# Conversion guards of attention-time weights moved to GpSimd in two steps, with shifts and joinings behind a unit's first maximum

## The chip, the cores and the metric

The kernel runs on one core of one Trainium2 chip. A time is device microseconds (us) of that core for one execution of the whole program. The number that is compared is the median over several executions: 718.2 us for the kernel before, from three runs (719.97, 717.71 and 718.2). The profile is of another execution of the same program, whose own time was 719.17 us.

## The reference

Three operators stand one behind the other.

```python
# 1. attention over 2 batches x 8 heads, 768 tokens, head size 64
q_bucket, k_bucket = sum over 6 bits of ((q @ proj > 0) * 2**bit), the same for k
mask = q_bucket[:, :, :, None] == k_bucket[:, :, None, :]
scores = np.where(mask, scale * q @ k.T, -1e9)
scores = scores - np.max(scores, axis=-1, keepdims=True)
attn = np.exp(scores); attn = attn / (attn.sum(-1) + 1e-9)
x = attn @ v                          # to 1536 tokens x 512
# 2. gated product, d_ff = 1536
x = (x @ w_a) * (x @ w_b) @ w_out
# 3. router and 8 experts, one expert for each token, d_ff = 1024
logits = normalised(x) @ normalised(expert_emb).T / tau
out[t] = gate[t] * relu(x[t] @ w1[e]) @ w2[e]      # e = argmax of the logits of token t
```

The weights reach the chip as 64-bit floats, in pairs of 32-bit words, and are made into two 32-bit parts (a high one and a small low one) on the chip. The products of stage 2 with the activations' high and low parts use them.

## The kernel before

**Stages.** Attention fills about the first 224 us of the span, the gated product runs from there to about 518 us, and the router and the experts fill the rest. The order of the instructions on each engine is written out by hand: Python code issues the work in program order, and each engine runs its own instructions in that order. The Tile layer adds the semaphore waits between engines.

**Attention.** The work is cut into 48 units (`units`): 8 pairs of heads, two heads in a pair, three groups of 256 queries in a head. The loop `for u in range(NU + 2)` issues, for unit u, in this order: the first row maximum on VectorE (`rowmax(u, 0)`, L278), its exponential on ScalarE (`expo`, L284), the reciprocal of the sums of the unit before (`recip(u - 1)`, L288, VectorE), the second maximum (`rowmax(u, 1)`), the normalising of the unit before (`normal(u - 1)`: a small `s` on VectorE in L294, a small `mc` and two 128x768 products `e` on GpSimd in L293 and L296), the first scores of the next unit on TensorE, the second exponential, the preparation of later heads, the transposing of unit u - 2 on VectorE (`turn`, L303), the second scores of the next unit, and a third of a head's product with the values (`pv`, L315). The scores live in a PSUM pool of two buffers, so the scores of a half wait for the exponential of the half two back.

**Hooks.** At fixed places of a unit the loop calls `hook(u, at)`: `at` 3 stands ahead of `turn`, 2 behind it, 0 behind the value products, 1 behind the loading of values, and 4 at the unit's end. A dictionary `plan` says what is issued there.

**Weights converted during attention.** The first two slices of `w_a`, `w_b` and `w_out` are converted while attention runs. `load_first` calls `split64`, which gives a `fetch` (a DMA on SyncE, L487) and seven steps: `rest` (a shift on VectorE, L492), `top` (a joining on VectorE, L495), `low` (ScalarE, L501), `add` (GpSimd, L506), `size` (ScalarE, L511), `guard` (VectorE, L517: the value is kept where its low word is large enough, else zero) and `parts` (a cast on ScalarE in L522, a subtraction on GpSimd in L523). `jobs[0..3]` are `w_a` and `w_b` of slice 0 and of slice 1, `outs[0..1]` are `w_out`. The table `places` names the unit of each of the seven steps of each job; `low` has m = 2, `guard` m = 5. The steps with m of 3, 4 and 6 stand at hook 3, the others at hook 4. The four jobs share the two buffers of `spare`, so that job 2 takes job 0's buffer and job 3 takes job 1's; the outs share the one buffer `late`.

**Fill-in products.** `fill` puts the first products of stage 2 into units 40, 43, 46, 47, 48, 51 and 52. Two halves of a product add up in one PSUM bank. Those of units 51 and 52 are read from their banks by ScalarE or VectorE (L601, L605) ahead of the first output product `yp` (L624), which takes the next bank in turn.

**Router.** For each token tile, `transpose_in` (T) turns the tile, and its eight logits come from a chain of products `lgp` (`route_logits`, R, L713) or, for three tiles at once, from one product `lgt` (`group_logits`, GL, L725) and three transposes `lgu` (`group_turn`, GT, L735). Tiles 9 to 11, the last ones, have T and R in a hand-written chain.

Of the kernel before, what the change touches and what calls it, by code (L numbers as in the profile page):

```python
# [25 lines left out]
class Kernel:  # L26
# [37 lines left out]
    def attention(self, xh, xl, pools, hook):  # L64
        nc = self.nc
# [306 lines left out]
        for u in range(NU + 2):  # L372
# [10 lines left out]
            if 0 <= u - 1 < NU:  # L383
                recip(u - 1)
            if act:
                rowmax(u, 1)
# [21 lines left out]
            if new < len(pairs):  # L408
                preps, held, held_kind = [kind(new, x) for x in (1, 0)], new, kind
# [46 lines left out]
class Experts:  # L456
# [16 lines left out]
    def split64(self, src, shape, dest, scratch=None):  # L473
# [40 lines left out]

        def guard():
            v = f32(T["v"])
            nc.vector.scalar_tensor_tensor(v, f32(T["lo"]), 2.0 ** -15, v, ALU.is_ge, ALU.mult)  # L517
# [7 lines left out]
        return fetch, [rest, top, low, add, size, guard, parts]  # L525
# [30 lines left out]
    def load_first(self, which, f, scratch):  # L556
# [15 lines left out]
        return self.split64(src, shape, dest, scratch)  # L572
# [145 lines left out]
    def group_logits(self, t):  # L718

        nc = self.nc  # L720
        yt = self.yT[t]
        q = self.rt.tile([128, 512], F32, tag="rt", name="lgt")
        for k in range(self.KD):
            rows = slice(32 * k, 32 * k + 32)
            nc.tensor.matmul(q[rows, :384], self.enT[:, k], yt[:, k], start=True, stop=True)  # L725
        ls = self.LS = self.sb.tile([128, self.DM], F32, tag="sq", name="lgs", bufs=1)
        nc.scalar.copy(ls[:, :384], q[:, :384])

    def group_turn(self, t):
# [4 lines left out]
        for m in range(3):  # L734
            nc.tensor.transpose(q[:, m * 128:(m + 1) * 128], self.LS[:, m * 128:(m + 1) * 128], self.K.ident)  # L735
        parts = q[:, :384].rearrange("p (m k e) -> p m e k", k=self.KD, e=32)
        nc.vector.tensor_reduce(self.lg[b][:, c:c + 3], parts[:, :, :self.E], axis=AX.X, op=ALU.add)
# [349 lines left out]
def tile_kernel(ctx, tc, q, k, v, proj, w_a, w_b, w_out, emb, tau, w1, w2, out, dbg=None):  # L1087
# [5 lines left out]
    with tc.manual_schedule():  # L1093
# [15 lines left out]
        with tc.tile_pool(name="conv", bufs=1, side="left") as X.conv, \  # L1109
# [7 lines left out]
            def late():  # L1117
                return sb.tile([128, 2 * S], F32, tag="raw", name="late", bufs=1)

            jobs = [X.load_first(w, f, spare) for f in range(2) for w in range(2)]  # L1120
            outs = [X.load_first(2, f, late) for f in range(2)]


            plan = {(-1, 0): [jobs[0][0], jobs[1][0]], (35, 1): [outs[0][0]], (45, 1): [outs[1][0]]}
            places = (
                (3, 4, 5, 6, 6, 7, 9), (8, 8, 9, 10, 12, 13, 15), (16, 17, 18, 21, 21, 22, 27), (20, 23, 24, 28, 30, 31, 33),
                (37, 38, 39, 40, 41, 41, 45), (NU, NU + 1, NU + 1, NU + 2, NU + 2, NU + 2, NU + 3),
            )
            for (_, steps), us in zip(jobs + outs, places):
                for m, u in enumerate(us):  # L1130
                    plan.setdefault((u, 3 if m in (3, 4, 6) else 4), []).append(steps[m])
            plan[13, 0], plan[16, 0] = [jobs[2][0]], [jobs[3][0]]
# [7 lines left out]
            def hook(u, at):  # L1140
# [5 lines left out]
                if at == 0:  # L1146
                    for n in range(fill.get(u, 0)):
                        t, f, w, half = first.pop(0)
                        if half == 0:
# [194 lines left out]
```

## Time and profile before

| | us |
|---|---|
| median of three runs | 718.2 |
| the profiled execution | 719.17 |
| its span (first to last instruction) | 717.3 |

| engine | busy us | share of the span | instructions |
|---|---|---|---|
| PE (TensorE) | 695.9 | 97% | 6802 |
| DVE (VectorE) | 463.8 | 65% | 672 |
| POOL (GpSimd) | 415.2 | 58% | 343 |
| ACT (ScalarE) | 354.8 | 49% | 659 |

The shares are means over three stages that differ. The clock granted to TensorE was 0.999 of full speed over the span. In rows of a timeline the first two numbers are the start and the duration in us; a bracket at the end is the idle time ahead of the instruction and what ended it. In rows that group instructions, the numbers behind the bar are the busy time in us, the mean of one in ns, and the idle time ahead with its releasers.

### The profile page before, as it was taken

What the parts mean: (1) busy time and instruction counts of PE and PEld (TensorE: products, weight loads), DVE (VectorE), ACT (ScalarE), POOL (GpSimd) and SP (SyncE); (2) the same over time, 40 slices, a digit from 0 to 9 for tenths busy, and PEclk for the clock granted to TensorE, in tenths of its full rate; (3) what the DMA queues carried; (4) which work ended last, traced back from release to release, by engine and by line L of the source; (5) the groups of instructions that cost most, each with busy time, mean ns of one, the idle gap of its engine ahead of it and who ended that gap; (6) DMA issues with size and microseconds to landing.
All of it is one profiled execution on the core that took longest, in us unless ns stands there. A gap on an engine that the chain in (4) does not pass through costs nothing.

```text
span 717.3 us, 16210 instructions
## 1 busy us (share of the span) xinstructions
PE 695.9 (97%) x6802; PEld 584.6 (82%) x6802; DVE 463.8 (65%) x672; ACT 354.8 (49%) x659; POOL 415.2 (58%) x343
## 2 busy tenths in 40 slices
PE   8799999999999999999999999999999999999996
PEld 5355655666688999999999999998899899989995
DVE  4999999999974726546556556325645766556650
ACT  4778888888663441121212112143546566556560
POOL 0658778887864645645626627454425666657651
PEclk9999999999999999999999999999999999999999
DMA  6947646644241311111302201633432866576510
GB/s 153 206 105 168 160 116 135 156 113 108 47 134 60 120 60 58 59 59 59 97 22 69 109 0 59 225 113 103 163 107 81 278 232 203 205 255 236 201 47 24
DMA packets 68443, 87.99 MB, mean 123 GB/s; under 512 B 28931, under 2 KB 41027, under 8 KB 68368
## 3 DMA queue, kind: packets, MB, share of 16 engines
q1 hardware_dynamic: 63728, 78.41, 37.5%
q0 software_dynamic: 2560, 7.34, 2.7%
q10 hardware_dynamic: 2080, 1.18, 0.6%
q8 instruction: 54, 0.88, 0.5%
q14 instruction: 21, 0.17, 0.1%
HBM read 75.52 MB, written 7.34 MB: 116 GB/s over the span
## 4 chain that ended last, share of the span: by engine, by line
PE 79%; DVE 11%; ACT 4%; issue 3%; DMA 3%; POOL 0%; SPq 0%; POOLq 0%; DVEq 0%
PE ab L592 25%; PE yp L624 14%; PE op L968 11%; PE hp L918 10%; PE pv L315 6%; DVE nm L278 5%; PE st L270 4%; DVE et L303 4%; ACT e L284 2%; PE hr L936 2%; PE part L592 2%; PE st L273 1%; PE xgt L895 1%; PE pv L592 1%; DMA late<-in_moe_w_out_dram 1%
## 5 line engine op out<-in xcount | busy, mean ns | idle before, releaser
L592 PE MATMUL ab<-xh,w 128*128 128x384 f32 x704 | 185.7, 338 | 0.0
L592 PEld LDWEIGHTS ab<-xh,w 128*128 128x128 f32 x704 | 127.7, 188 | 2.0 <-issue 1.2
L296 POOL TENSOR_SCALAR e<-e,s,mc 128x768 f32<-128x768 f32 x96 | 93.5, 984 | 43.0 <-ACT e L284 33.0
L592 PE MATMUL ab<-xl,w 128*128 128x384 f32 x352 | 118.3, 336 | 0.0
L607 POOL TENSOR_TENSOR g<-a,g 128x384 fp32r<-128x384 f32 x48 | 53.5, 1115 | 102.4 <-ACT g L606 102.4
L874 POOL TENSOR_TENSOR w<-raw,w 128x1024 fp32r<-128x1024 f32 x36 | 88.2, 2454 | 37.2 <-ACT w L873 35.7
L624 PE MATMUL yp<-w,g 128*128 128x512 f32 x432 | 103.0, 391 | 0.7 <-DVE a L605 0.7
L284 ACT ACTIVATE e<-st,nm 128x768 f32<-128x768 f32 x96 | 85.8, 899 | 32.4 <-DVE r L288 22.2
L278 DVE TENSOR_REDUCE nm<-st 128x1 f32<-128x768 f32 x96 | 89.6, 938 | 8.9 <-PE st L273 8.4
L624 PEld LDWEIGHTS yp<-w,g 128*128 128x128 f32 x432 | 80.3, 188 | 15.9 <-DVE a L605 1.0
L270 PE MATMUL st<-ks,qs 64*128 64x384 f32 x192 | 83.2, 513 | 5.4 <-ACT e L284 5.4
L270 PE MATMUL st<-k,q 64*128 64x384 f32 x192 | 83.8, 517 | 3.6 <-ACT e L284 3.3
L303 DVE STREAM_TRANSPOSE et<-e 128x1536 f32<-128x1536 f32 x48 | 84.9, 1769 | 0.0
L968 PE MATMUL op<-w,hth 128*128 128x512 f32 x256 | 80.8, 397 | 0.0
L918 PE MATMUL hp<-xgh,w 128*128 128x256 f32 x448 | 80.7, 281 | 0.0
L606 ACT CAST g<-a 128x384 fp32r<-128x384 f32 x48 | 24.7, 515 | 111.0 <-DVE a L605 111.0
L874 DVE TENSOR_TENSOR w<-raw,w 128x1024 fp32r<-128x1024 f32 x28 | 67.4, 2406 | 13.5 <-ACT w L873 13.5
L315 PEld LDWEIGHTS pv<-et,vr 32*64 32x64 f32 x3072 | 60.2, 130 | 18.2 <-issue 9.4
L315 PE MATMUL pv<-et,vr 32*64 32x192 f32 x3072 | 72.5, 326 | 2.3 <-ACT q L128 1.6
L918 PEld LDWEIGHTS hp<-xgh,w 128*128 128x128 f32 x448 | 69.2, 188 | 0.3
L601 ACT COPY a<-ab 128x384 f32<-128x384 f32 x44 | 21.0, 478 | 95.3 <-PE ab L592 94.1
L629 DVE TENSOR_TENSOR y<-yp,y 128x512 f32<-128x512 f32 x60 | 41.5, 692 | 39.2 <-PE yp L624 39.2
(217 smaller groups left out, 1260.4 us busy)
## 6 DMA issues: line engine op xcount, KB each, us to landing
raw<-in_moe_w_dram SPq DMA_DIRECT2D x32, 1024.0 KB, 5.4
vr<-in_v_dram SPq DMA_DIRECT2D x64, 192.0 KB, 3.8
raw<-in_moe_w_a_dram SPq DMA_DIRECT2D x5, 1024.0 KB, 5.0
raw<-in_moe_w_b_dram SPq DMA_DIRECT2D x5, 1024.0 KB, 5.1
raw<-in_moe_w_out_dram SPq DMA_DIRECT2D x5, 1024.0 KB, 5.0
raw<-in_k_dram SPq DMA_DIRECT2D x16, 192.0 KB, 4.0
qs<-q SPq DMA_DIRECT2D x15, 192.0 KB, 3.8
raw<-in_q_dram SPq DMA_DIRECT2D x14, 192.0 KB, 4.3
```

The lines of the kernel that those rows point to most:

```text
L270: nc.tensor.matmul(st[:, n, :H2], q[d, ql], k[d], start=True, stop=False, tile_position=(64 * n, 0))
L278: nc.vector.tensor_reduce(NM[u][:, t:t + 1], ST[u, t][:, :, :H2], axis=AX.XY, op=ALU.max, negate=True)
L284: nc.scalar.activation(halves(E[u][:, t]), ST.pop((u, t))[:, :, :H2], AF.Exp, bias=NM[u][:, t:t + 1], accum_out=SU[u][:, t:t + 1])
L296: nc.gpsimd.tensor_scalar(E[u][:, t], E[u][:, t], r[:, t:t + 1], c[:, t:t + 1], ALU.mult, ALU.add)
L303: nc.vector.transpose(ET[h][:, :, 2 * g:2 * g + 2].rearrange("p b c s -> p c b s"), E.pop(u).rearrange("p c (b s) -> p c b s", s=32),)
L315: nc.tensor.matmul(pvb[a // 2][m:m + 64, a % 2, :NC * 32], v[d], et[d, n].rearrange("p c s -> p (c s)"), start=(n < 2), stop=(n >= NB32 - ...
L592: nc.tensor.matmul(p[:, :384], w[:, k, fs], x[:, k, cols], start=(k == 0 and n == 0), stop=(k == self.KD - 1 and n == 2),)
L607: nc.gpsimd.tensor_tensor(gl[:, f], a, f32(gh[:, f]), ALU.subtract)
L624: nc.tensor.matmul(p, g[:, f, rows], w[:, f], start=(n == 0), stop=(n == 5))
L874: eng.tensor_tensor(l, raw, f32(h), ALU.subtract)
L918: nc.tensor.matmul(p[:, :256], w[:, k, fs], x[:, k], start=(n == 0), stop=(n == 3 * self.KD - 1))
L968: nc.tensor.matmul(p, h[:, 2 * n + f, rows], w[:, f], start=(n == 0 and f == 0 and m == 0), stop=(n == 3 and f == 1 and m == 2),)
```

## The change

The guard of the weights that are converted during attention gets another form where its engine is GpSimd: `mask` turns the low word into 0 or 1 in place, and `guard` multiplies the value by it. Five of the six guards take this form; that of `outs[1]` stays on VectorE. A new hook 5 stands between the reciprocal and the second maximum, and `rest` and `top` go there. The table `places` has eight columns and other units. The fetch of job 3 goes from hook 0 of unit 16 to hook 0 of unit 21, and that of `outs[1]` from (45, 1) to (46, 1). The two preparations of signs are issued in the other order. One more PSUM bank is taken ahead of the products of unit 51. In the router, tiles 9 and 10 get their logits from one `group_logits` of 256 columns and two transposes in the place of two `route_logits`.

```diff
--- before.py
+++ after.py
@@ -382,6 +382,7 @@
                 expo(u, 0)
             if 0 <= u - 1 < NU:
                 recip(u - 1)
+            hook(u, 5)
             if act:
                 rowmax(u, 1)
             if 0 <= u - 1 < NU:
@@ -406,7 +407,7 @@
             if u + 1 < NU:
                 scores(u + 1, 1)
             if new < len(pairs):
-                preps, held, held_kind = [kind(new, x) for x in (1, 0)], new, kind
+                preps, held, held_kind = [kind(new, x) for x in ((1, 0) if kind is turned else (0, 1))], new, kind
             elif s != 1 and u >= 5:
                 n = (u - 5) % 3
                 pv((u - 5) // 3, range(12 * n, 12 * n + 12))
@@ -470,7 +471,7 @@
         self.yT, self.sel, self.mx, self.rps, self.HS, self.RW = ({} for _ in range(6))
 
 
-    def split64(self, src, shape, dest, scratch=None):
+    def split64(self, src, shape, dest, scratch=None, eng=None):
 
         nc = self.nc
         n = shape[0] * shape[1]
@@ -512,8 +513,15 @@
             else:
                 nc.vector.tensor_scalar(T["lo"], T["hi"], 0x7FFFFFFF, None, ALU.bitwise_and)
 
+        def mask():
+            if eng is nc.gpsimd:
+                eng.tensor_scalar(f32(T["lo"]), f32(T["lo"]), 2.0 ** -15, 1.0, ALU.is_ge, ALU.mult)
+
         def guard():
             v = f32(T["v"])
+            if eng is nc.gpsimd:
+                eng.tensor_tensor(v, v, f32(T["lo"]), ALU.mult)
+                return
             nc.vector.scalar_tensor_tensor(v, f32(T["lo"]), 2.0 ** -15, v, ALU.is_ge, ALU.mult)
 
         def parts():
@@ -522,7 +530,7 @@
             nc.scalar.copy(h, v)
             nc.gpsimd.tensor_tensor(l, v, f32(h), ALU.subtract)
 
-        return fetch, [rest, top, low, add, size, guard, parts]
+        return fetch, [rest, top, low, add, size] + ([mask] if eng else []) + [guard, parts]
 
     def parts(self, shape):
 
@@ -553,7 +561,7 @@
             jobs.append(self.split64(src[:, rows], (n, shape[1]), dest, scratch))
         return jobs
 
-    def load_first(self, which, f, scratch):
+    def load_first(self, which, f, scratch, eng):
 
         K = self.K
         w32 = [w.bitcast(I32) for w in (K.w_a, K.w_b, K.w_out)][which]
@@ -569,7 +577,7 @@
                 self.WG[0, which] = self.parts(whole)
             return [t[:, :, 128 * f:128 * f + 128] if which < 2 else t[:, f:f + 1] for t in self.WG[0, which]]
 
-        return self.split64(src, shape, dest, scratch)
+        return self.split64(src, shape, dest, scratch, eng)
 
 
     def gated_products(self, c, t, f, which, half, psum=None, held=None):
@@ -715,26 +723,27 @@
             )
         nc.vector.tensor_copy(self.lg[b][:, c], q[:, :self.E])
 
-    def group_logits(self, t):
-
-        nc = self.nc
-        yt = self.yT[t]
+    def group_logits(self, t, m=3):
+
+        nc = self.nc
+        n = 128 * m
+        yt = self.yT[t][:, :, :n]
         q = self.rt.tile([128, 512], F32, tag="rt", name="lgt")
         for k in range(self.KD):
             rows = slice(32 * k, 32 * k + 32)
-            nc.tensor.matmul(q[rows, :384], self.enT[:, k], yt[:, k], start=True, stop=True)
+            nc.tensor.matmul(q[rows, :n], self.enT[:, k], yt[:, k], start=True, stop=True)
         ls = self.LS = self.sb.tile([128, self.DM], F32, tag="sq", name="lgs", bufs=1)
-        nc.scalar.copy(ls[:, :384], q[:, :384])
-
-    def group_turn(self, t):
+        nc.scalar.copy(ls[:, :n], q[:, :n])
+
+    def group_turn(self, t, n=3):
 
         nc = self.nc
         b, c = divmod(3 * t, self.TB)
         q = self.rt.tile([128, 512], F32, tag="rt", name="lgu")
-        for m in range(3):
+        for m in range(n):
             nc.tensor.transpose(q[:, m * 128:(m + 1) * 128], self.LS[:, m * 128:(m + 1) * 128], self.K.ident)
-        parts = q[:, :384].rearrange("p (m k e) -> p m e k", k=self.KD, e=32)
-        nc.vector.tensor_reduce(self.lg[b][:, c:c + 3], parts[:, :, :self.E], axis=AX.X, op=ALU.add)
+        parts = q[:, :128 * n].rearrange("p (m k e) -> p m e k", k=self.KD, e=32)
+        nc.vector.tensor_reduce(self.lg[b][:, c:c + n], parts[:, :, :self.E], axis=AX.X, op=ALU.add)
 
     def wide(self, t):
         return t.rearrange("p (t e) -> p t e", e=1).to_broadcast([128, self.TB, self.E])
@@ -1117,19 +1126,20 @@
             def late():
                 return sb.tile([128, 2 * S], F32, tag="raw", name="late", bufs=1)
 
-            jobs = [X.load_first(w, f, spare) for f in range(2) for w in range(2)]
-            outs = [X.load_first(2, f, late) for f in range(2)]
-
-
-            plan = {(-1, 0): [jobs[0][0], jobs[1][0]], (35, 1): [outs[0][0]], (45, 1): [outs[1][0]]}
+            jobs = [X.load_first(w, f, spare, nc.gpsimd) for f in range(2) for w in range(2)]
+            outs = [X.load_first(2, f, late, (nc.gpsimd, nc.vector)[f]) for f in range(2)]
+
+
+            plan = {(-1, 0): [jobs[0][0], jobs[1][0]], (35, 1): [outs[0][0]], (46, 1): [outs[1][0]]}
             places = (
-                (3, 4, 5, 6, 6, 7, 9), (8, 8, 9, 10, 12, 13, 15), (16, 17, 18, 21, 21, 22, 27), (20, 23, 24, 28, 30, 31, 33),
-                (37, 38, 39, 40, 41, 41, 45), (NU, NU + 1, NU + 1, NU + 2, NU + 2, NU + 2, NU + 3),
+                (3, 4, 5, 6, 6, 6, 7, 9), (9, 10, 12, 15, 15, 15, 16, 21),
+                (16, 21, 21, 22, 24, 24, 27, 33), (22, 27, 27, 28, 30, 30, 34, 39),
+                (37, 38, 39, 40, 41, 41, 45, 46), (NU, NU + 1, NU + 1, NU + 2, NU + 2, NU + 2, NU + 2, NU + 3),
             )
             for (_, steps), us in zip(jobs + outs, places):
                 for m, u in enumerate(us):
-                    plan.setdefault((u, 3 if m in (3, 4, 6) else 4), []).append(steps[m])
-            plan[13, 0], plan[16, 0] = [jobs[2][0]], [jobs[3][0]]
+                    plan.setdefault((u, 3 if m in (3, 4, 7) or m == 6 and u < NU else 5 if m < 2 and u < NU else 4), []).append(steps[m])
+            plan[13, 0], plan[21, 0] = [jobs[2][0]], [jobs[3][0]]
             first = [(t, f, w, h) for t in range(2) for f in range(2) for w in range(2) for h in range(2)]
 
 
@@ -1147,6 +1157,8 @@
                     for n in range(fill.get(u, 0)):
                         t, f, w, half = first.pop(0)
                         if half == 0:
+                            if (u, n) == (NU + 3, 0):
+                                K.bank()
                             X.part = K.banks[(2, 0)[n // 2]] if u < NU - 1 else K.bank()
                         X.gated_products(0, t, f, w, half, X.part, held if u < NU + 2 else None)
 
@@ -1287,7 +1299,7 @@
         after(("o", L, 3, 0), X.transpose_in, 0, 0)
         after(("o", L, 3, 0), X.gather, 1, 0)
         chain(("o", L, 3, 1), [
-            (T, 9), [(T, 10), (R, 9)], [(T, 11), (X.route_norm, 1), (R, 10)], [(R, 11), (X.route_choose, 1)],
+            (T, 9), (T, 10), [(T, 11), (GL, 3, 2), (X.route_norm, 1)], [(R, 11), (GT, 3, 2), (X.route_choose, 1)],
         ])
         after(("t", 0, 0, 0), X.route_places, 1)
         chain(("e", 0, 0, 0), [[(X.route_slots, 1), (X.gather, 0, 1)]])
```

**VectorE, units 21 to 23.** Here `spare_1270` (before) and `spare_1640` (after) are job 3's buffer, `spare_1055` and `spare_1054` are job 2's. `nm` is the pair of maxima of a unit, of which each has two rows. Before, from the first maximum of unit 20:

```order
L278 TENSOR_REDUCE nm_1486<-st_1458 128x1 [waits PE_49]
L288 RECIPROCAL r_1491<-su_1446 128x2 [waits Activation_49]
L278 TENSOR_REDUCE nm_1486<-st_1471 128x1 [waits PE_49]
L294 SCALAR_TENSOR_TENSOR s2_1495<-nm_1444,r_1491 128x2 [waits DVE_49]
L303 STREAM_TRANSPOSE et_1512<-e_1364 128x2x24x32 [waits Pool_49]
L492 TENSOR_SCALAR spare_1270<-spare_1270 128x512 [waits DMAHW5_49]
L278 TENSOR_REDUCE nm_1569<-st_1500 128x1 [waits PE_49]
L288 RECIPROCAL r_1574<-su_1488 128x2 [waits Activation_49]
L278 TENSOR_REDUCE nm_1569<-st_1514 128x1 [waits PE_49]
L294 SCALAR_TENSOR_TENSOR s2_1578<-nm_1486,r_1574 128x2 [waits DVE_49]
L303 STREAM_TRANSPOSE et_1512<-e_1447 128x2x24x32 [waits Pool_49]
L278 TENSOR_REDUCE nm_1650<-st_1583 128x1 [waits PE_49]
```

After, from the first maximum of unit 21:

```order
L278 TENSOR_REDUCE nm_1562<-st_1494 128x1 [waits PE_49]
L288 RECIPROCAL r_1567<-su_1482 128x2 [waits Activation_49]
L496 SCALAR_TENSOR_TENSOR spare_1054<-spare_1054 128x512
L278 TENSOR_REDUCE nm_1562<-st_1508 128x1 [waits PE_49]
L294 SCALAR_TENSOR_TENSOR s2_1572<-nm_1480,r_1567 128x2 [waits DVE_49]
L303 STREAM_TRANSPOSE et_1506<-e_1441 128x2x24x32 [waits Pool_49]
L278 TENSOR_REDUCE nm_1649<-st_1577 128x1 [waits PE_49]
L288 RECIPROCAL r_1654<-su_1564 128x2 [waits Activation_49]
L493 TENSOR_SCALAR spare_1640<-spare_1640 128x512 [waits DMAHW3_49,Pool_49]
L278 TENSOR_REDUCE nm_1649<-st_1587 128x1 [waits PE_49]
L294 SCALAR_TENSOR_TENSOR s2_1659<-nm_1562,r_1654 128x2 [waits DVE_49]
L303 STREAM_TRANSPOSE et_1506<-e_1483 128x2x24x32
```

Before, job 3's shift follows the transpose of unit 20 and waits for its load alone. After, job 3's shift stands between the two maxima of unit 22 (`nm_1649`) and waits for its load and for GpSimd; job 2's joining stands in unit 21.

**SyncE, around job 3's load.** `vr` are values, `qg` the query signs, `raw` keys and queries of a later pair. Before:

```order
L94 DMA vr_1219<-in_v_dram 32x4x384 [waits DMAHW4_49]
L487 DMA spare_1270<-in_moe_w_b_dram 128x4x256 [waits DMAHW5_49,DVE_49,Pool_49]
L87 DMA raw_1293<-in_k_dram 128x6x64 [waits DMAHW6_49,PE_49]
L87 DMA raw_1293<-in_q_dram 128x6x64 [waits DMAHW7_49]
L87 DMA raw_1293<-in_k_dram 128x6x64 [waits DMAHW0_49]
L87 DMA raw_1293<-in_q_dram 128x6x64 [waits DMAHW1_49]
```

After:

```order
L240 DMA qg_1471<-qf_1470 64x384 [waits DMAHW1_49,Activation_49]
L240 DMA qg_1471<-qf_1470 64x384 [waits DMAHW2_49]
L488 DMA spare_1640<-in_moe_w_b_dram 128x4x256 [waits DMAHW3_49,DVE_49,Pool_49]
L94 DMA vr_1642<-in_v_dram 32x4x384 [waits DMAHW4_49,PE_49]
L94 DMA vr_1642<-in_v_dram 32x4x384 [waits DMAHW5_49]
L94 DMA vr_1642<-in_v_dram 32x4x384 [waits DMAHW6_49]
L94 DMA vr_1642<-in_v_dram 32x4x384 [waits DMAHW7_49]
L87 DMA raw_1717<-in_k_dram 128x6x64 [waits DMAHW0_49,PE_49]
```

The load of job 3 has moved from behind the values of unit 15 to behind `qg` of unit 20, ahead of the values issued in unit 21; in both kernels it waits for GpSimd's last use of the buffer.

**GpSimd, units 20 and 21.** `spare_217` is job 1's buffer, `w_1583` the low part of job 1's weight. Before:

```order
L347 TENSOR_TENSOR xl0_100<-xp_1035,xh0_98 128x384 [waits Activation_49]
L293 TENSOR_SCALAR mc_1577<-nm_1486 128x2
L296 TENSOR_SCALAR e_1489<-e_1489,s2_1578,mc_1577 128x768 [waits DVE_49,Activation_49,Pool_49]
L296 TENSOR_SCALAR e_1489<-e_1489,s2_1578,mc_1577 128x768 [waits Activation_49]
L506 TENSOR_TENSOR spare_1055<-spare_1055,r64_1442 128x512 [waits DMAHW4_49]
L293 TENSOR_SCALAR mc_1658<-nm_1569 128x2
```

After:

```order
L347 TENSOR_TENSOR xl0_100<-xp_1034,xh0_98 128x384 [waits Activation_49]
L293 TENSOR_SCALAR mc_1571<-nm_1480 128x2
L296 TENSOR_SCALAR e_1483<-e_1483,s2_1572,mc_1571 128x768 [waits DVE_49,Activation_49,Pool_49]
L296 TENSOR_SCALAR e_1483<-e_1483,s2_1572,mc_1571 128x768 [waits Activation_49]
L531 TENSOR_TENSOR w_1583<-spare_217,w_1583 128x4x128 [waits Activation_49]
L293 TENSOR_SCALAR mc_1658<-nm_1562 128x2
```

In unit 21 the add of job 2 stood behind the two products `e`; the subtraction of job 1 (its `parts`) stands there now, the last use of the buffer that job 3's load takes. Before, that subtraction stood in unit 15, behind `e_1063`.

## Rows read from the trace of the kernel before

**Rows 1.** Busy time by stretch: us, busy PE, PEld, DVE, ACT, POOL, granted clock, DMA share, GB/s.

```profile
20.00:170.00 150.00, 139.78 (x2781) 86.65 (x2787) 144.75 (x200) 124.14 (x257) 113.15 (x140) 1.00 0.61 142
225.00:485.00 260.00, 260.00 (x1392) 243.84 (x1391) 135.84 (x182) 67.33 (x124) 138.24 (x79) 1.00 0.23 77
```

**Rows 2.** Timeline of DVE, from the transpose in unit 21 to that in unit 25.

```profile
99.31 1.76 DVE L303 STREAM_TRANSPOSE et<-e 128x1536 f32<-128x1536 f32 x1
101.00 0.91 DVE L278 TENSOR_REDUCE nm<-st 128x1 f32<-128x768 f32 x1
101.85 0.14 DVE L288 RECIPROCAL r<-su 128x2 f32<-128x2 f32 x1
...
102.83 1.77 DVE L303 STREAM_TRANSPOSE et<-e 128x1536 f32<-128x1536 f32 x1
104.52 1.14 DVE L517 SCALAR_TENSOR_TENSOR spare<-spare 128x512 f32<-128x512 f32 x1
...
109.14 1.06 DVE L495 SCALAR_TENSOR_TENSOR spare<-spare 128x512 int32<-128x512 int32 x1
...
115.51 1.77 DVE L303 STREAM_TRANSPOSE et<-e 128x1536 f32<-128x1536 f32 x1
```

**Rows 3.** Timeline of DVE: transposes in units 7, 10, 28, 31 and 34, and one guard.

```profile
41.45 1.77 DVE L303 STREAM_TRANSPOSE et<-e 128x1536 f32<-128x1536 f32 x1
...
54.53 1.77 DVE L303 STREAM_TRANSPOSE et<-e 128x1536 f32<-128x1536 f32 x1
...
126.87 1.77 DVE L303 STREAM_TRANSPOSE et<-e 128x1536 f32<-128x1536 f32 x1
...
138.46 1.77 DVE L303 STREAM_TRANSPOSE et<-e 128x1536 f32<-128x1536 f32 x1
140.16 1.07 DVE L517 SCALAR_TENSOR_TENSOR spare<-spare 128x512 f32<-128x512 f32 x1
...
150.24 1.77 DVE L303 STREAM_TRANSPOSE et<-e 128x1536 f32<-128x1536 f32 x1
```

**Rows 4.** Timeline of POOL, in unit 21: job 2's add, behind the two products.

```profile
101.49 1.28 POOL L506 TENSOR_TENSOR spare<-spare,r 128x512 int32<-128x512 int32 x1
```

**Rows 5.** DMA issues of jobs 2 and 3: KB each, us from issue to landing.

```profile
spare<-in_moe_w_a_dram SPq DMA_DIRECT2D x1, 512.0 KB, 6.4
...
spare<-in_moe_w_b_dram SPq DMA_DIRECT2D x1, 512.0 KB, 5.5
```

**Rows 6.** Groups by line and shape: GpSimd's normalising, and the cast of a late weight.

```profile
L296 POOL TENSOR_SCALAR e<-e,s,mc 128x768 f32<-128x768 f32 x96 | 93.5, 984 | 43.0 <-ACT e L284 33.0 <-DVE s L294 9.4 <-POOL mc L293 0.2
L522 ACT CAST w<-late 128x512 fp32r<-128x512 f32 x2 | 1.2, 614 | 0.0
```

**Rows 7.** Timeline of DVE and of POOL, around the one long `s` of attention.

```profile
193.96 0.77 DVE L294 SCALAR_TENSOR_TENSOR s<-nm,r 128x2 f32<-128x2 f32 x1
```

```profile
193.71 1.00 POOL L347 TENSOR_TENSOR xl<-xp,xh 128x384 fp32r<-128x384 f32 x1
```

**Rows 8.** Busy time by stretch at the end, columns as in rows 1.

```profile
711.00:713.00 2.00, 0.26 (x2) 0.00 (x0) 0.00 (x0) 0.69 (x1) 0.69 (x1) 1.00 0.00 0
713.00:715.00 2.00, 0.00 (x0) 0.00 (x0) 0.00 (x0) 0.00 (x0) 0.29 (x1) 1.00 0.26 97
715.00:717.30 2.30, 0.00 (x0) 0.00 (x0) 0.00 (x0) 0.00 (x0) 0.00 (x0) 0.55 0.00 0
```

**Rows 9.** Timeline of PE: the first output product, and the router's last logits.

```profile
224.69 4.35 PE L624 MATMUL yp<-w,g 128*128 128x512 f32 x18 [0.72 <-DVE a L605]
...
514.47 0.85 PE L725 MATMUL lgt<-yt,enT 128*32 128x384 f32 x8
...
517.12 0.49 PE L735 MATMUL lgu<-ident,lgs 128*128 128x128 f32 x3
...
518.23 1.06 PE L713 MATMUL lgp<-enT,yt 128*128 128x8 f32 x8 [0.18 <-DVE lg L737]
...
521.08 0.96 PE L713 MATMUL lgp<-enT,yt 128*128 128x8 f32 x8
```

## The prediction

> **What bounds the kernel now.** I read the busy times by stretch first. The reader is to see two regimes. In the gated product PE is busy for all of 260 us, and an edit counts there only for the PE time that it takes or gives. In attention PE is busy 139.78 of 150 us, but DVE 144.75 [rows 1]: DVE sets the pace. Next comes the timeline of DVE, for what a unit costs it. From the transpose at 99.31 to the maximum at 101.00 are 1.69 us, and from there to the next transpose at 102.83 are 1.83 [rows 2]; a unit without other work takes 3.52, three take 10.56. In rows the three units from 126.87 to 138.46, with no conversion step on DVE, took 11.59 [rows 3], so about 1.0 us in three units is waiting for others, and a first conversion step can hide in it. Three units with one step (138.46 to 150.24) took 11.78, with two (102.83 to 115.51) 12.68 [rows 2, 3], with three (41.45 to 54.53) 13.08 [rows 3]. So the steps cost 0.19, 1.09 and 1.49 together. Last come the DMA landings and GpSimd's timeline, for what the moved load waits for.
>
> **The change part by part.**
>
> *Five guards leave DVE; shifts and joinings move.* Counting by groups of three units, before has six groups with one step, three with two and one with three: 6 x 0.19 + 3 x 1.09 + 1.49 = 5.9 us for 15 steps. After has ten steps, four groups with one and three with two: 4 x 0.19 + 3 x 1.09 = 4.0. That gives -1.9. The ends are five steps at the price of a first one (5 x 0.19 = -1.0) and five at the whole duration of a guard (1.07 and 1.14 in two rows, -5.5 [rows 2, 3]). I take -2.4, a little beyond the count: the joining that stays took 1.06 us beside GpSimd's products [rows 2], and behind the first maximum it should meet them less often.
>
> *Masks and products on GpSimd.* No row shows a mask. From the normalising, 984 ns for 768 elements [rows 6], 512 elements are 0.66 us as an estimate; the add of the same size took 1.28 [rows 4], the upper end. What it costs is what it holds up. The two products and an add end at 102.77, 3.46 us behind the transpose at 99.31 [rows 2, 4], and the small `s` of DVE starts just there (102.77 is the transpose at 102.83 less its 0.06). In units 6 and 15 add and mask stand together, so GpSimd is busy 0.66 to 1.28 us beyond that point. The row to read is the long `s`: 0.77 us, from 193.96 to 194.73, while a subtraction of GpSimd ran from 193.71 to 194.71 [rows 7]. So `s` ended with GpSimd's instruction. The Trainium skill (SBUF — State Buffer, section "SBUF: two separate sides") says that GpSimd and a VectorE instruction with two SBUF inputs share a port pair that whichever comes first holds for its whole instruction. The row agrees; by that rule each mask that overlaps `s` costs its remainder, and without it the masks would cost nothing. From the rows alone the cost lies between 0 and 2 x 1.28 = 2.6; I take +0.8, near two remainders of a short mask with part of it absorbed.
>
> *Job 3's load.* This is the largest term. The shift of job 3 stands between the two maxima of unit 22, where DVE arrives after the reciprocal, at about 101.94 on the clock of before (the maximum at 101.00 is unit 22's first) [rows 2]. It needs the load, which SyncE issues in unit 21 but which waits until GpSimd has read job 1's value for the last time. That subtraction now stands in unit 21 behind two products, where before the add ends at 102.77 [rows 4]; I give it the same end. The two loads of this size took 6.4 and 5.5 us from issue to landing [rows 5]. So the data are there at 108.3 to 109.2, and DVE, with the second maximum behind the shift, stands for 6.3 to 7.2 us; I take 6.8. Behind the shift on DVE wait the second maximum, `s` and the transpose; ACT waits for that maximum with its exponential, PE for the exponential with its next scores, GpSimd for `s`: nothing covers it. Of the waits of others (1.0 in three units, above) the stall can swallow some; I take 0.7 off: +6.1. The values of the next head are queued on SyncE behind the waiting load, but are read units later; 0.
>
> *The clock.* PE has next to nothing to do in the stall. At the end of the span PE did its last 0.26 us of work after 711.00, the granted clock was 1.00 until 715.00, and 0.55 in the last 2.3 us [rows 8], which is the lower level of 1.2 GHz for most of that stretch. The stall is about as long as this whole end (711.26 to 717.3). The Trainium skill (TensorE: Matmul & The Clock Gate, "What's actually happening") calls the lower level the default, which activity lifts; by that the cost below is real, without it it is nothing. PE's work is 0.93 of the time in attention [rows 1], so at half the clock a unit of 3.52 us takes up to 3.3 more. I take half a unit's worth, +1.7, between 0 and 3.3.
>
> *The tail.* The last guard of the late weights and its cast move: the cast, 614 ns [rows 6], now stands on ACT ahead of the exponentials of unit 47, in a stretch in which products of stage 2 already fill PE; 0 to +0.6, and I take +0.6, since PE has no other slack there. The extra PSUM bank takes away the wait of 0.72 us ahead of the first output product [rows 9]; the second half of its input comes from the same DVE instruction, so I take -0.4 of at most -0.72. In the router two chains of `lgp` go: 1.06 and 0.96 us, with 0.18 of waiting before the first. One `lgt` of 256 columns and two `lgu` come: 0.85 and 0.49 us at three tiles [rows 9], two thirds of it is 0.89, all of it 1.34. So -0.9 to -1.3; I take -0.9. The exchanged signs: each still has a unit's time, 0.
>
> The sum: -2.4 + 0.8 + 6.1 + 1.7 + 0.6 - 0.4 - 0.9 = +5.5 us. On the profiled execution that is 724.7; the median shown, 718.2, lies 0.97 lower, so the forecast is 723.7.
>
> **The rivals.**
>
> *The clock stays up, or its fall is hidden.* DVE sets the pace in attention, and PE at half speed for a moment may cost little. Then +3.8: 722.0. For it speaks that PE is busy less than DVE; against it, that 0.93 at half the clock doesn't fit into a unit.
>
> *Most of the stall is given back.* If each guard was worth its whole 1.1 us, and the clock costs nothing: -5.5 + 0.8 + 6.1 - 0.4 - 0.9 + 0.3 = +0.4: 718.6, no change. The price of a first step (0.19) speaks against it.
>
> *GpSimd becomes the bound.* Masks of 1.28 us and products beside normalising hold `s` in more units: +2.6 in the place of +0.8, 725.5. GpSimd was busy 113.15 of 150 us [rows 1], which speaks against a lasting jam.
>
> *No stall (the other side).* If GpSimd's last read of job 1's buffer comes a whole unit earlier against DVE, or the load is in place because the shift comes late, the term of 6.1 and the clock go: -2.4 + 0.8 + 0.6 - 0.4 - 0.9 = -2.3: 715.9, faster. It decides from the point at which the landing takes under 1 us after DVE's arrival; the landings of 5.5 and 6.4 stand against it, for it only that the order shows waits and no times.
>
> **How the numbers follow.** The forecast has 0.55, the clock without cost 0.22, GpSimd as the bound 0.08, the stall given back 0.10, no stall 0.05. A measurement of this kernel can tell about 0.3% from no change, 2.15 us: 716.05 to 720.35 is the same. Faster is the case without a stall: 0.05. The same is the case given back, and a little of the second: 0.11. Slower is the rest: 0.84. The likeliest case by itself reaches from 721.0 (guards at -5.1 with the rest as taken) to 726.5 (stall at 7.2, clock at 3.3, masks at 1.6). The range for 8 times in 10 reaches down into the case given back and up into GpSimd's: 719.9 to 727.0.
>
> **What would show it.** In the profile after, DVE's timeline has one gap of about 6 to 7 us ahead of the shift of `spare` around 102 us, ended by the DMA of `spare`, and SyncE's issue of it waits for GpSimd's subtraction. PE, ACT and GpSimd are idle in the same stretch, and the granted clock of the stretch behind it is under 1. Attention's end lies about 6 us later than 224 us, and the gated product and the experts take what they took. Groups of three units without the stall are about as long as before or shorter. `s` is longer in units 6 to 7 and 15 to 16. The forecast is wrong if the load lands before DVE arrives, if the stall is under 4 us, or if attention outside it changes by more than 3 us.

## The result, and the profile after

The changed kernel took 729.34 us in the median of six runs, against 718.86 of the kernel before: a ratio of 1.014 (95% interval 1.0117 to 1.0164). It is slower, as forecast, but by 10.5 us, where 5.5 were forecast (723.7, range to 727.0). The profiled execution took 729.39 us, with a span of 727.5 and a mean granted clock of 0.992.

The forecast gap is there. DVE, timeline of unit 22 in the kernel after; the bracket is the idle time ahead and what ended it:

```profile
98.93 1.76 DVE L303 STREAM_TRANSPOSE et<-e 128x1536 f32<-128x1536 f32 x1
100.62 0.91 DVE L278 TENSOR_REDUCE nm<-st 128x1 f32<-128x768 f32 x1
101.47 0.14 DVE L288 RECIPROCAL r<-su 128x2 f32<-128x2 f32 x1
106.03 0.43 DVE L493 TENSOR_SCALAR spare<-spare 128x512 int32<-128x512 int32 x1 [4.42 <-DMA spare<-in_moe_w_b_dram]
106.37 0.95 DVE L278 TENSOR_REDUCE nm<-st 128x1 f32<-128x768 f32 x1
...
107.31 1.77 DVE L303 STREAM_TRANSPOSE et<-e 128x1536 f32<-128x1536 f32 x1
```

GpSimd's last use of the buffer and SyncE's issue behind it, in the timelines of POOL and SP, and the load's time to landing:

```profile
101.11 1.28 POOL L531 TENSOR_TENSOR w<-spare,w 128x512 fp32r<-128x512 f32 x1
...
102.42 0.40 SPq L488 DMA_DIRECT2D spare<-in_moe_w_b_dram  x1
```

```profile
spare<-in_moe_w_b_dram SPq DMA_DIRECT2D x1, 512.0 KB, 3.5
```

The subtraction ends 3.46 us behind the transpose at 98.93, where the add of before ended behind its own [rows 2, 4], and the issue follows at once. The load then took 3.5 us; the two of before took 5.5 and 6.4 [rows 5]. So DVE stood for 4.42 us, not 6.8. TensorE lost its clock behind it. Busy time by stretch, columns as in rows 1:

```profile
102.00:104.00 2.00, 2.00 (x70) 1.28 (x54) 0.00 (x0) 0.62 (x2) 0.62 (x2) 1.00 0.21 47
104.00:106.00 2.00, 0.24 (x4) 0.00 (x0) 0.00 (x0) 0.00 (x0) 0.00 (x0) 1.00 1.04 358
106.00:108.00 2.00, 0.00 (x0) 0.00 (x0) 1.97 (x4) 0.64 (x1) 0.44 (x1) 0.97 1.09 219
108.00:110.00 2.00, 1.60 (x6) 0.66 (x6) 1.99 (x3) 1.93 (x6) 2.00 (x3) 0.50 0.26 44
110.00:112.00 2.00, 2.00 (x12) 1.70 (x9) 1.59 (x3) 1.90 (x4) 1.32 (x3) 0.50 0.00 0
112.00:114.00 2.00, 2.00 (x10) 1.37 (x10) 1.12 (x1) 1.91 (x4) 2.00 (x3) 0.50 0.00 0
114.00:116.00 2.00, 2.00 (x28) 0.91 (x32) 1.03 (x3) 0.00 (x0) 0.77 (x2) 0.83 0.66 150
```

At 0.50 the clock is at its lower level, 1.2 GHz, for some 6 us; PE is now the busy engine and DVE waits (1.12 and 1.03 of 2 us busy).

A second gap was not forecast. The timeline of SP and of DVE in units 36 and 37 of the kernel after:

```profile
164.59 1.77 DVE L303 STREAM_TRANSPOSE et<-e 128x1536 f32<-128x1536 f32 x1
...
167.71 0.16 DVE L288 RECIPROCAL r<-su 128x2 f32<-128x2 f32 x1
170.58 0.43 DVE L493 TENSOR_SCALAR late<-late 128x512 int32<-128x512 int32 x1 [2.71 <-DMA late<-in_moe_w_out_dram]
```

```profile
165.35 0.53 SPq L488 DMA_DIRECT2D late<-in_moe_w_out_dram  x1
```

The same place in the kernel before, where the shift stood at the end of the unit and shows no wait, and the load in the chain that ended last:

```profile
157.72 1.77 DVE L303 STREAM_TRANSPOSE et<-e 128x1536 f32<-128x1536 f32 x1
...
163.71 0.63 DVE L492 TENSOR_SCALAR late<-late 128x512 int32<-128x512 int32 x1
```

```profile
158.48 5.21 DMA late<-in_moe_w_out_dram
...
163.71 0.63 DVE late L492
```

In both, the load is issued 0.76 us behind a transpose. Before, the shift came 5.99 us behind that transpose; after, DVE arrives 3.28 us behind it (167.87 less 164.59) and starts at 5.99. The load took 5.21 us in both traces. Before, it landed at 163.69, and the shift started at 163.71: nothing was to spare, and the new hook took 2.7 us away from it. So the trace of before did show this load, in its chain, though not as a wait of DVE.

The masks took longer than the prediction's upper end for them, 1.28 us. Groups by line and shape of the kernel after:

```profile
L518 POOL TENSOR_SCALAR spare<-spare 128x512 f32<-128x512 f32 x4 | 8.4, 2090 | 0.3
L523 POOL TENSOR_TENSOR spare<-spare 128x512 f32<-128x512 f32 x4 | 5.2, 1290 | 0.0
L294 DVE SCALAR_TENSOR_TENSOR s<-nm,r 128x2 f32<-128x2 f32 x48 | 12.0, 249 | 0.0
```

The two longest `s` (1.25 us and this one) stand beside products, not masks. Timelines of POOL and of DVE of the kernel after:

```profile
45.34 1.29 POOL L523 TENSOR_TENSOR spare<-spare 128x512 f32<-128x512 f32 x1
...
77.85 2.15 POOL L518 TENSOR_SCALAR spare<-spare 128x512 f32<-128x512 f32 x1
```

```profile
45.56 1.09 DVE L294 SCALAR_TENSOR_TENSOR s<-nm,r 128x2 f32<-128x2 f32 x1
...
78.84 0.14 DVE L294 SCALAR_TENSOR_TENSOR s<-nm,r 128x2 f32<-128x2 f32 x1
```

The first `s` ended with the product (46.65 and 46.63); the second ran inside a mask and took no longer than an undisturbed one.

The tail: the first output product waits as before, and the router's new products.

```profile
235.18 4.35 PE L632 MATMUL yp<-w,g 128*128 128x512 f32 x18 [0.72 <-DVE a L613]
...
530.94 0.64 PE L734 MATMUL lgt<-yt,enT 128*32 128x256 f32 x8
...
533.82 0.41 PE L744 MATMUL lgu<-ident,lgs 128*128 128x128 f32 x2
```

By stretches between the same instructions, after less before, in us: to the transpose of unit 21 -0.4; to unit 28's +7.3; to unit 36's 0.0; to unit 39's +2.4; to the first output product +1.2; the rest -0.3. The sum is the 10.2 by which the spans differ.

### The profile page after: what moved, and what is told of

The parts are those of the page before. It is cut to its first block, busy times and chain, and to the rows that moved or that the text cites. A ratio compares the mean times of both kernels' runs of the same rounds, so it can differ in the third digit from the quotient of the medians.

```text
span 727.5 us, 16214 instructions
## 1 busy us (share of the span) xinstructions
PE 700.8 (96%) x6796; PEld 585.5 (80%) x6796; DVE 458.7 (63%) x666; ACT 356.8 (49%) x660; POOL 430.3 (59%) x353
## 4 chain that ended last, share of the span: by engine, by line
PE 76%; DVE 9%; ACT 6%; issue 3%; DMA 3%; POOL 2%; SPq 0%; POOLq 0%; ACTq 0%; DVEq 0%
PE ab L600 24%; PE yp L632 13%; PE op L977 11%; PE hp L927 10%; PE pv L315 6%; PE st L270 4%; DVE nm L278 4%; ACT e L284 3%; DVE et L303 2%; PE part L600 2%; PE st L273 1%; PE hr L945 1%; PE xgt L904 1%; ACT xp L335 1%; DMA late<-in_moe_w_out_dram 1%
## 5 line engine op out<-in xcount | busy, mean ns | idle before, releaser
L270 PE MATMUL st<-ks,qs 64*128 64x384 f32 x192 | 85.6, 527 | 8.0 <-ACT e L284 7.5
L270 PE MATMUL st<-k,q 64*128 64x384 f32 x192 | 86.2, 530 | 4.4 <-ACT e L284 3.9
L883 DVE TENSOR_TENSOR w<-raw,w 128x1024 fp32r<-128x1024 f32 x28 | 64.7, 2310 | 14.6 <-ACT w L882 14.4
L600 PEld LDWEIGHTS ab<-xl,w 128*128 128x128 f32 x352 | 66.3, 188 | 0.8
```

Of the source, the lines that this page charges most:

```text
L270: nc.tensor.matmul(st[:, n, :H2], q[d, ql], k[d], start=True, stop=False, tile_position=(64 * n, 0))
L600: nc.tensor.matmul(p[:, :384], w[:, k, fs], x[:, k, cols], start=(k == 0 and n == 0), stop=(k == self.KD - 1 and n == 2),)
L883: eng.tensor_tensor(l, raw, f32(h), ALU.subtract)
```

## The experiments

Times are medians beside those of the kernel before on the same chip; the ratio has its 95% interval.

**Each wait taken away, and both.** `a1_shift_job3_later` has the first edit, `a2_shift_out0_later` the second, `a3_both_later` both.

```diff
-                (16, 21, 21, 22, 24, 24, 27, 33), (22, 27, 27, 28, 30, 30, 34, 39),
+                (16, 21, 21, 22, 24, 24, 27, 33), (24, 27, 27, 28, 30, 30, 34, 39),
...
-                (37, 38, 39, 40, 41, 41, 45, 46),
+                (38, 39, 39, 40, 41, 41, 45, 46),
```

> The changed kernel with one number of the table altered: job 3's shift stands in unit 24 and not in unit 22 (its load still issued in unit 21). Theory (two waits of VectorE for a load, each followed by some us at half the clock): the gap of 4.42 us in unit 22 and the half clock behind it go, the gap of 2.71 us in unit 37 stays; 729.3 - 4.4 - 2.5 to 3 = about 722. Rival 1 (the loss is the gap alone, the clock costs nothing): about 725. Rival 2 (the masks and products on GpSimd are what costs): 728 to 729, since units that wait for the load would wait for GpSimd anyway.

> The changed kernel with the shift of the first w_out slice in unit 38 and not in unit 37, and its joining in unit 39 and not in unit 38. Theory (two waits for a load, each with its clock): the gap of 2.71 us in unit 37 goes and with it the half clock from 172.7 to 176; about 729.3 - 2.7 - 1 = 725.5. Rival (the second gap is hidden further on, where products of stage 2 fill PE): no change, 729.

> Both tables altered, so that no shift waits for its load; guards, masks, router and bank as in the changed kernel. Theory (the two waits and their clock are the whole loss): granted clock 0.999 as before, and a time between 716 and 719, since the parts of the change that gain (router, bank, fewer steps on VectorE) then stand alone. Rival (masks on GpSimd hold up `s`): 720 to 724 with the clock up.

Measured: a1 722.38 us against 719.46 (1.0051, 1.0032 to 1.0071); a2 725.18 (1.008, 1.006 to 1.0101); a3 719.16 (0.9995, 0.9983 to 1.0008). The first wait is worth some 7 us, the second some 4, each give or take 2 by the intervals, and without them nothing of the loss is left. That the masks are the loss is refuted; so is a hidden second gap. What a3 does not show is the gain that the sum gave to the rest of the change: it was expected at 716 to 719.

**TensorE kept busy in the gaps**, with the gaps left as they are. In `a4_busy_pe_in_gaps` the scores of two units are computed several times:

```diff
+            for _ in range({(23, 0): 4, (38, 0): 3}.get((u, t), 1)):
             for n, d in enumerate(rows):
...
```

> The changed kernel, with the four products of the first scores of unit 23 issued four times and those of unit 38 three times, each time anew from zero, so that TensorE has work in both gaps and the result is that of one. Both gaps of VectorE stay. Theory (behind each gap the half clock costs time of its own): the clock stays at 1.00 behind both gaps and the time is 3 to 4 us under the changed kernel, about 725.5. Rival (VectorE sets the pace and the clock costs nothing): 729 to 730.

Measured: 727.19 us against 719.46 (1.0111, 1.009 to 1.0132), 2.15 less than the changed kernel. The two intervals overlap (the changed kernel's is 1.0117 to 1.0164), so the medians alone do not show a gain; what follows rests on the traces, one execution each. That of a4 was the shortest of its six, 725.38 us at a mean clock of 0.998; the other five have 0.994 to 0.997. DVE's first gap was 4.78 us in it, and the clock stayed up behind it. Stretches of a4:

```profile
106.00:108.00 2.00, 0.19 (x4) 0.00 (x0) 2.00 (x4) 0.76 (x1) 0.55 (x1) 1.00 1.07 213
108.00:110.00 2.00, 1.71 (x12) 1.04 (x12) 2.00 (x4) 1.93 (x6) 2.00 (x3) 1.00 0.10 17
```

The transposes of units 21, 28, 36 and 39, of a4:

```profile
98.46 1.76 DVE L304 STREAM_TRANSPOSE et<-e 128x1536 f32<-128x1536 f32 x1
...
131.22 1.76 DVE L304 STREAM_TRANSPOSE et<-e 128x1536 f32<-128x1536 f32 x1
...
161.76 1.77 DVE L304 STREAM_TRANSPOSE et<-e 128x1536 f32<-128x1536 f32 x1
...
177.08 1.76 DVE L304 STREAM_TRANSPOSE et<-e 128x1536 f32<-128x1536 f32 x1
```

and of a3, without gaps:

```profile
97.82 1.76 DVE L303 STREAM_TRANSPOSE et<-e 128x1536 f32<-128x1536 f32 x1
...
126.64 1.76 DVE L303 STREAM_TRANSPOSE et<-e 128x1536 f32<-128x1536 f32 x1
...
157.75 1.77 DVE L303 STREAM_TRANSPOSE et<-e 128x1536 f32<-128x1536 f32 x1
...
170.79 1.77 DVE L303 STREAM_TRANSPOSE et<-e 128x1536 f32<-128x1536 f32 x1
```

From unit 21 to 28, a3 takes 28.82 us, a4 32.76, and the changed kernel 34.83 (98.93 to 133.76). So a gap of 4.8 us costs 3.9 with the clock up (4.3 against c2 below, which takes 28.47), and the half clock behind the gap 2.1 more. In a2, whose clock was low for about 3.5 us and not some 6, they take 34.06: 1.3 more than a4. From unit 36 to 39 a3, a4 and the changed kernel take 13.04, 15.32 and 15.38, and a1 16.04: there the gap costs 2.3 and its half clock 0.1 to 0.7. The clock is a cost of its own at the first gap, and a small one at the second, which has fewer us at the lower level. The theory holds in kind; 3 to 4 us was too much.

The kernel before takes 27.56 us from unit 21 to 28, so 1.3 of the 7.3 lost there are neither gap nor clock. The versions with the new table and no gap in this stretch all take 28.4 to 29.0, b1 below, without masks, too; b2 and b3 below, which keep the old places of loads and guards, take 27.78 and 27.75. Which of the moved steps or loads costs this was not tried.

**The load's place in the queue.** In `b4_load_behind_values` the load goes behind the four loads of values:

```diff
-            plan[13, 0], plan[21, 0] = [jobs[2][0]], [jobs[3][0]]
+            plan[13, 0], plan[21, 1] = [jobs[2][0]], [jobs[3][0]]
```

> The changed kernel, with job 3's load issued behind the values of unit 21 and not ahead of them. Theory (the load took 3.5 us and not the 5.5 to 6.4 of before because it was alone in the queue, the four loads of values behind it): it lands 5 to 6 us after its issue, which comes 1 to 2 us later; the gap of unit 22 grows from 4.4 to 7 to 8 us, the time to 732 to 734. Rival (landing time depends on the half of the day, not on the queue): 3.5 us again, gap 5 to 6 us, 730 to 731.

Measured: 732.22 us against 719.15 (1.0177, 1.0151 to 1.0203). SP's and DVE's timelines of b4, and the landing:

```profile
103.19 1.74 SPq L94 DMA_DIRECT2D vr<-in_v_dram  x4
105.04 0.39 SPq L488 DMA_DIRECT2D spare<-in_moe_w_b_dram  x1
```

```profile
110.27 0.43 DVE L493 TENSOR_SCALAR spare<-spare 128x512 int32<-128x512 int32 x1 [8.81 <-DMA spare<-in_moe_w_b_dram]
```

```profile
spare<-in_moe_w_b_dram SPq DMA_DIRECT2D x1, 512.0 KB, 5.1
```

With 0.77 MB of values just ahead of it the same load took 5.1 us, in the changed kernel, ahead of them, 3.5. The gap was longer than I expected, since the issue came 2.6 us later than in the changed kernel. But the load takes other times in the changed kernel's place as well: 3.7 us in a1 and a3, 3.9 in a4, 4.1 in a2, and 5.1 in c4 below. So b4 does not show that the order in the queue is what made the load quick.

**A shorter gap.** `c4_short_gap` is a2 with job 3's shift in unit 23 (the 24 of a1's edit is a 23).

> a2_shift_out0_later with job 3's shift in unit 23, one unit and not two behind the changed kernel's place, so that VectorE meets the load some 3.5 to 3.7 us later and waits about 1 us in the place of 4.4 to 5. Theory (the half clock hangs on the length of TensorE's gap): no half clock, a gap of 0.5 to 1.5 us that others' waits swallow in part: 719.5 to 720.5. Rival (any wait of VectorE for a load brings the clock down): 721.5 to 722.5.

Measured: 719.44 us against 718.53 (1.0015, 1.0006 to 1.0025). The load's issue and landing, the gap, and the clock around it:

```profile
100.42 0.40 SPq L488 DMA_DIRECT2D spare<-in_moe_w_b_dram  x1
```

```profile
spare<-in_moe_w_b_dram SPq DMA_DIRECT2D x1, 512.0 KB, 5.1
```

```profile
105.66 0.43 DVE L493 TENSOR_SCALAR spare<-spare 128x512 int32<-128x512 int32 x1 [2.35 <-DMA spare<-in_moe_w_b_dram]
```

```profile
106.00:108.00 2.00, 0.00 (x0) 0.00 (x0) 2.00 (x4) 1.01 (x3) 0.78 (x1) 1.00 1.27 180
108.00:110.00 2.00, 1.64 (x34) 0.97 (x39) 2.00 (x4) 1.71 (x3) 2.00 (x3) 1.00 1.37 217
```

2.35 us of waiting, at the full clock, cost about 1 us by the medians and 1.7 by the traces (30.48 us from unit 21 to 28, a3 28.82). The wait was longer than expected, since the load took 5.1 us; the time is at the lower end of what was expected. A wait for a load does not bring the clock down by itself.

**The rest of the change.** `b1_guards_on_vector` is a3 with `nc.vector` for `nc.gpsimd` in the two lines that call `load_first`. `b3_hook5_only` is the kernel before with only hook 5: each `rest` and `top` stands there in the unit behind its old one, as (20, 23, ...) to (21, 24, ...).

> The kernel with both shifts later (a3_both_later), with all guards on VectorE again as one instruction each, in the units and at the hook of the changed kernel; no mask. Theory (the masks and products on GpSimd give back about what the guards on VectorE cost, since a3 is level with before): within 0.3% of a3, 718 to 721, with the small `s` short again in units 6 to 7 and a guard of 0.7 to 1.1 us on VectorE in its place. Rival 1 (a guard on VectorE costs its whole 1.1 us, five of them 5): 723 to 724. Rival 2 (masks cost more than guards): 716 to 717.

> The kernel before with only the new hook: each shift and joining of attention goes from the end of its unit to the place between the reciprocal and the second maximum of the next unit; guards stay on VectorE at their places, loads too. Theory (a shift or joining there meets GpSimd less): shifts of 0.43 us in the place of 0.63 to 0.81, in all 0 to -1.5 us: 718 to 719.5. Rival (the second maximum behind it is the one that PE waits for, through the exponential): +2 to +4, 721.5 to 723.5.

Measured: b1 719.25 us, b3 719.36, both against 719.15 (0.9997, 0.9984 to 1.0011, and 0.9998, 0.9979 to 1.0017). Neither the engine of the guards nor the place of the shifts can be told from no change. In a3 the group of `s` reads:

```profile
L294 DVE SCALAR_TENSOR_TENSOR s<-nm,r 128x2 f32<-128x2 f32 x48 | 10.6, 221 | 0.0
```

In b1 the `s` take 8.2 us in all, in the kernel before 8.0: with masks and products on GpSimd `s` gives back 2.4 us of what the guards free on DVE. In all, guards on DVE and masks on GpSimd cost the same, to within some 1.3 us by the two intervals.

`b2_router_bank_only` is the kernel before with `group_logits(t, m)`, `group_turn(t, n)`, the new chain and the call of `K.bank()` as in the change's diff.

> The kernel before with only two parts of the change: the router's logits of tiles 9 and 10 by one product of 256 columns and two transposes, and the extra PSUM bank. By my sum -0.9 and -0.4: 718.2 beside 719.5. The traces so far say: the router -0.8, the bank 0, since the wait of 0.72 us ahead of the first output product stands in a3 and in the changed kernel too; 718.7. Rival: no change at all, because the last choice of experts comes later by what the products save.

Measured: 717.35 us against 719.15 (0.9972, 0.9956 to 0.9989). It is the only version here that beats the kernel before, and it beats the changed one by 12. In its trace the wait ahead of the first output product is still 0.72 us and the way from there to the experts' first `op` product is 302.1 us, against 303.1 before: the router gives 1.0 and the bank nothing that the trace shows. This way takes 302.1 or 302.7 us in every version with the new router (302.7 in the changed kernel), 303.1 in the kernel before and 303.7 in b3. The median fell by 1.8, more than the 0.8 expected; the trace does not show where the rest lies. On the same chip b1, which has this router too, takes 1.9 more than b2: the other parts of the change cost about what the router gives, part of it between units 21 and 28 (above).

**Signs and the late cast**, on a3. `c1_signs_as_before` has the first edit, `c2_late_cast_early` the second, `c3_signs_and_cast` both:

```diff
-                preps, held, held_kind = [kind(new, x) for x in ((1, 0) if kind is turned else (0, 1))], new, kind
+                preps, held, held_kind = [kind(new, x) for x in (1, 0)], new, kind
...
-                (38, 39, 39, 40, 41, 41, 45, 46),
+                (38, 39, 39, 40, 41, 41, 43, 45),
```

> The kernel with both shifts later (a3_both_later), with the two preparations of signs in the order of the kernel before. Theory (a3 is level with before, although its router is 1 to 2 us quicker, because the rest of the change costs 1 to 2 us; the signs are no part of that): within 0.2% of a3, 718 to 720.5. Rival (the swap puts the query signs' copy earlier and the key signs' later, and PE's scores wait for them): 717 to 718.

> a3_both_later, with the guard of the first w_out slice in unit 43 and its parts in unit 45 in the place of 45 and 46, so that its cast is not on ScalarE behind the copies of unit 46. Theory (the cast of 0.62 us there delays the exponentials of unit 47 and by them the value product): the stretch from the transpose of unit 47 to the first output product goes back from 23.5 to 22.8 us, 718.4 to 718.7. Rival (the second half of that stretch waits for other things): 719.2, as a3.

> Both edits of c1_signs_as_before and c2_late_cast_early on a3_both_later. Theory: the sum of the two, 718 to 719; it beats the kernel before by the router alone (719.3 - 0.8), and not the kernel before with router and bank alone (717.35). Rival (the signs matter): under 717.3.

Measured: c1 718.72 us, c2 718.70 and c3 718.46, against 718.53 (0.9985 to 1.0016, 0.9983 to 1.0008, 0.999 to 1.0011). None can be told from no change by its time. From the transpose of unit 47 to the first output product are 22.58 us in c2 (202.01 to 224.59), 23.51 in a3 (202.06 to 225.57) and 22.76 in the kernel before (201.93 to [rows 9]). That looks like the cast, but is not: b2 and b3, in which the cast stands where it stood before, take 23.51 as well, and in c2 the stretch from unit 39 to 47 is 0.6 longer than in a3 (31.89 and 31.27). That the late cast costs anything is not shown.

## Why the prediction was wrong

- *The load of job 3, +6.1.* The mechanism was right: the wait chain from GpSimd's subtraction to SyncE to DVE, and the place. The size was not. The landing times of 5.5 and 6.4 us came from two loads issued behind others [rows 5]; here it was 3.5, and 3.7 to 5.1 in the same place of other versions. What sets it is open. The gap was 4.42 us, in cost about 4 for a like gap in a4.
- *The step that failed: "Five guards leave DVE; shifts and joinings move".* It priced all ten moved steps as DVE time, -2.4, and only for job 3 was it asked whether the load had landed. The shift of the first `w_out` slice moved 2.7 us forward as well, and its load lands when the old place came. That wait stood at nothing, without a reason. a2 shows some 4 us for it, the traces 2.3 for the gap and 0.1 to 0.7 for its clock. This is the largest part of the miss. The stretches up to the first output product, without that from unit 21 to 28, grew by 3.2 us in all, past the 3 that the prediction named as a sign of being wrong.
- *The clock, +1.7.* 1.3 to 2.1 at the first gap and 0.1 to 0.7 at the second, by the traces: the rival that it costs nothing is refuted there. The size was about right, but it was picked from the middle of 0 to 3.3, so that is luck; and by the prediction's own numbers a unit at half the clock takes 3.0 more (2 x 0.93 x 3.52 less 3.52), not 3.3. By the rule of the Trainium skill (TensorE: Matmul & The Clock Gate, "What's actually happening"), that activity lifts the clock from its default, a busy TensorE in the gap should hold the clock up. The trace of a4 agrees: 1.00 behind both gaps.
- *Guards and masks, -2.4 and +0.8.* Together 0 (a3, b1). The masks took 2.0 to 2.2 us, not 0.66 to 1.28. A mask works in place on every second word; a product reads the same words and took 1.29, so reading them does not explain it by itself; whether the writing or the comparing does was not tried. That each mask that overlaps `s` costs its remainder did not come out: inside masks `s` took 0.14 to 0.48 us (the kernel after and a3) and ended well ahead of them, and the two longest, 1.09 and 1.25 us, ended with products. The joinings did not get shorter behind the first maximum either: 1.06 us in a3, 0.97 before. The rival "GpSimd becomes the bound" is refuted, since b1 without masks takes the same.
- *The tail.* The cast, +0.6: not shown, by b2 and b3. The router, -0.9: -1.0 by b2's trace, -0.4 in the changed kernel's. The bank, -0.4: nothing; the product waits for the same instruction as before.
- *The sum.* Taking the measured sizes, 7.0 (a1) + 4.2 (a2) + 0 for the rest is 11.2, against 10.5 measured, well within their noise. The range missed because its upper end was the likeliest case with a longer stall, a dearer clock and dearer masks, and held no room for a second wait of the kind.

## What to carry to other kernels

When an instruction is moved forward, look at everything that it waits for, each instance by itself, and not only the one whose load is moved too: a load that lands just in time shows no wait on its engine, but it can stand in the chain that ended last, as here. Take a landing time as a range: one load, in one place, took 3.5 to 5.1 us. Price a gap of the pacing engine with what TensorE does behind it, since the lost clock came to a quarter to a half of the first gap again.

## What the runs showed of the hardware

- A 512 KB load, with four loads of values issued behind it and none just ahead, landed 3.5 us after its issue in the kernel after, 3.7 in a1 and a3, 3.9 in a4, 4.1 in a2 and 5.1 in c4; in b4, with 0.77 MB just issued ahead, 5.1. What sets this is open.
- GpSimd's compare and multiply on 512 floats in place, on every second word, took 2.0 to 2.2 us, a product of the same size that reads those words 1.29.
- A small two-input `s` of VectorE ended with GpSimd's product when it started beside one (1.09 us), and took 0.14 to 0.48 us inside compares and multiplies of 2.0 to 2.2 us, without lasting to their end.
- The clock did not follow the length of PE's gap alone. In the kernel after, PE waited 4.16 us ahead of the scores at 108.40 and 2.20 us ahead of those at 172.95, and fell to the lower level behind both; in c4 it waited 2.35 us, and the clock stayed at 1.00. What sets this is open. PE's timeline and the stretches behind the second gap, of the kernel after:

```profile
108.40 1.00 PE L270 MATMUL st<-ks,qs 64*128 64x384 f32 x1 [4.16 <-ACT e L284]
...
172.95 1.00 PE L270 MATMUL st<-k,q 64*128 64x384 f32 x1 [2.20 <-ACT e L284]
```

```profile
170.00:172.00 2.00, 0.75 (x6) 0.10 (x2) 1.42 (x4) 0.09 (x1) 0.00 (x0) 1.00 0.37 102
172.00:174.00 2.00, 1.05 (x4) 0.66 (x6) 2.00 (x2) 1.98 (x5) 1.86 (x2) 0.68 0.66 191
174.00:176.00 2.00, 2.00 (x8) 0.53 (x6) 2.00 (x4) 1.96 (x5) 1.60 (x3) 0.50 0.47 113
```

and of c4:

```profile
108.04 0.59 PE L270 MATMUL st<-k,q 64*128 64x384 f32 x1 [2.35 <-ACT e L284]
```
